# Routing before the values, four marks a step, eight early splits: one change to a fused attention and mixture kernel

## The chip, the cores and the metric

The kernel runs on one core of a Trainium2 chip. The metric is device time in microseconds (us). TensorE is called PE below, VectorE DVE, ScalarE ACT, GpSimd POOL, and SyncE SP.

## The reference, cut to what matters

```
scores = where(0 <= i - j < 64, q k^T / 8, -1e9);  x = softmax(scores) v           # B=4, H=8, S=576, D=64
x -> [2304, 512];  noisy = x @ w_gate + log1p(exp(x @ w_noise)) * noise             # 8 experts
top 2 of noisy per token, softmax of the two -> top2_w
y = sum over the two of top2_w * (relu(x @ w1[e]) @ w2[e])                           # w1 512x1024, w2 1024x512
h = y @ w_in;  g = h if h >= 1, 0 if h <= -1, else (h + 1)^2 / 4;  out = g @ w_out   # w_in 512x2048
```

## The kernel before, in words

There are 18 tiles of 128 tokens. A tile is cut into two units, so attention has 36 units and the loop at its heart calls `step(u)` for u = 0 to 36. One step writes down work of several units, and each engine executes its share in the order in which it is written (`manual_schedule`: nothing is reordered). In an even step PE gets the scores of the next tile (L282 mask, L291), the transposes of an older tile's output (`Ex`, L347), the transposes of the unit's probabilities (`C`, L313), the products (`place`, L557) and the 32 matmuls of probabilities and values (`Dm`, L327). In an odd step it gets `C`, `place` and the gate logits (`Gm`, L365). DVE has the row maxima (`top`, L298, two in an even step), the division of the values by their sums (in `Dm`, L332, L333 and L335, which makes the tile `x`), the routing, and the subtraction that splits a weight chunk into a high and a low part (`split_w`, L148; ACT makes the high part at L147).

Routing goes by groups of six tiles. `route(g)` is a generator: `advance` runs it up to a `yield` of 1 or 2, and then the rest waits for the next step. Its pieces are the noisy logits (L426 to L450), the largest eight and their indices (L454, L457), the one-hot choices (L460 to L478), the positions (PE, L482 to L486: how many tokens before this one chose the same expert), the slot numbers (L491 to L505) and then twelve pairs of marks a group: `ohr` (L510, DVE) and `ohe` (L517 on DVE for odd tiles, L520 on ACT for even ones). `MARKS` says how many pairs one call of `advance` takes. `place` in the next call multiplies each pair on PE (L557) and adds the product to one PSUM tile, the list of token numbers by expert.

After the 24 products of the first two groups, `early` reads that list (L385 to L401), and POOL gathers three blocks of 128 rows (`xg0a`, L650) with which expert 0 starts while the third group is still routed. The blocks are transposed (L672) and split (L675 ACT, L676 DVE `xlo0a`) behind steps 35 and 36. Then the experts run: `mm1` (L763), `act_relu` (L769 ACT, L770 DVE `hl`), `mm2` (L803), by weight chunks. `tail` routes the third group between the chunks of expert 0, two calls a chunk, then makes the rest of the list (`finish_ids`) and gathers the other two blocks of expert 0 (`xg0b`); the first block of expert 1 (`xge`) is gathered at the first chunk of the unit `0b`.

`EW` weight chunks are loaded and split during attention, half a chunk a step, one every `LS` steps; `SPLITS[0]` splits the next ones at chunks `F0` and on of expert 0. Three `raw` tiles take the loads.

```
n_early = 2 * gstart[EARLY]                              # 24 products
calm = 2 if g < EARLY - 1 else 0                         # in route: groups 1 and 2 go on at once
if state["first"] or nids[0] < n_early: return           # in early
for b in range((0, 1, NA)[max(u - NU + 2, 0)]):          # behind steps 35 and 36
    if ("0a", b) in gat: xpose("0a", b, NA, Sb[b])
```

Of the kernel before, what the change touches and what calls it, by code (L numbers as in the profile page):

```python
# [28 lines left out]
NT = N // P  # L29
# [6 lines left out]
GROUPS = [6, 6, 6]  # L36
EARLY = 2
NA = 3
MARKS, TAIL = (2, 6), 6
Y0, LOOK = 3, 1  # L40
PTB = 3
EW, L0, LS, F0 = 10, 1, 3, 4
G2 = [2, 4, 4, 4, 4]
NCE = E * NF
MID = N // 2
# [8 lines left out]
def fused_kernel(ctx, tc, qT, kT, v, wg, noise, wcat, out, wd=None):  # L54
# [17 lines left out]
    att, rte, ffn = ExitStack(), ExitStack(), ExitStack()  # L72
    wk = rte.enter_context(tc.tile_pool(name="wk", bufs=2, side="right"))
    gp = rte.enter_context(tc.tile_pool(name="gp", bufs=2, side="right"))
    oh = rte.enter_context(tc.tile_pool(name="oh", bufs=8, side="right"))
    ac = rte.enter_context(tc.tile_pool(name="ac", bufs=1, side="right"))
    qk = att.enter_context(tc.tile_pool(name="qk", bufs=2))
    vp = att.enter_context(tc.tile_pool(name="vp", bufs=4))
# [125 lines left out]
    for s in (0, 64):  # L204
        nc.gpsimd.affine_select(out=id64[s:s + 64, :], in_=id64[s:s + 64, :], compare_op=ALU.not_equal, fill=1.0,
                                base=0, pattern=[[-1, 64]], channel_multiplier=1)
        m = m0[s:s + 64]
# [94 lines left out]
    def soft(u):  # L302
        sb, nb = Sb[u % 3], mxs.pop(u)
        p = wk.tile([P, 4, P], F32, tag="p", name=f"p{u}", bufs=4)
        for g in range(4):
            nc.scalar.activation(p[:, g, :], sb[:, g * P:g * P + P], AF.Exp, bias=nb[:, g:g + 1], scale=0.125)
        pr[u] = p
# [106 lines left out]
    def route(g):  # L414
# [40 lines left out]
        yield calm  # L455
        for a in range(T):
            nc.vector.max_index(out=ix[:, a, :], in_max=mx8[:, t0 + a, :], in_values=ny[:, a, :])  # L457
        yield calm
        ixf = tl("ixf", [P, T, 2])
        nc.vector.tensor_copy(ixf, ix[:, :, 0:2])  # L460
        yield 0
# [130 lines left out]
    def logits(i, u):  # L592
        Gm(i, u)
        g, t = tile_group[i]
        if t == GROUPS[g] - 1:
            live.append(route(g))
            next(live[-1])

    def step(u):
        for c in range(EW):  # L600
            if u == L0 + LS * c:
                load_raw(c)
        if u + 2 < NU:
            if (u + 2) % 4 == 0 and (u + 2) // 4 + 1 < NT // 2:
                load_qk((u + 2) // 4 + 1)
                keys_before((u + 2) // 4 + 1)
            if (u + 1) % 2 == 0 and (u + 1) // 2 + 1 < NT:
                load_v((u + 1) // 2 + 1)


        m = u // 2
        if u % 2 == 0:
            if u + 2 < NU:
                A(m + 1)
            if 0 <= m - 2 < NT:
                Ex(m - 2, u)
        if u < NU:
            C(u)
        if u % 2 == 0 and u + 2 < NU:
            top(u + 2)  # L620
            top(u + 3)
        if u + 2 < NU:
            soft(u + 2)
        place()
        early()
        if 0 <= u - 1 < NU:
            Dm(u - 1)
        if u % 2 == 1 and 0 <= m - 2 < NT:
            logits(m - 2, u)
        advance(MARKS[u > NU - 10])  # L630

        for c in range(EW):
            for h in range(2):
                if u == L0 + LS * c + 3 + h:
                    split_w(c, h)
            if u == L0 + LS * c + 4 and c >= EW - 2:
                load_raw(c + 2)
# [57 lines left out]
    def tail():  # L695
        logits(NT - 2, NU + 1)
        Ex(NT - 1, NU + 1)
        advance(TAIL)
        yield
        logits(NT - 1, NU + 1)  # L700
        while live or oq or pq:
            place()
            advance(TAIL)
            yield
        finish_ids([(NA, NB), (0, NA), (NB, E * JB)])
        count()
        rte.close()
        pool["xp"] = ffn.enter_context(tc.tile_pool(name="xp", bufs=2, reuse_waits="tile", side="right"))
        for b in range(units[1]["nb"]):
            prep_gather(units[1], b)  # L710
            yield

    def count():
        cnt = bank[6][:, CNT:CNT + E]
# [248 lines left out]
    for s in range(len(seq)):  # L963
        ui, n = seq[s]
        un = units[ui]
        f = n - un["ch"][0]
        nxt = units[ui + 1] if ui + 1 < len(units) else None
        last = f == len(un["ch"]) - 1
        decode = 1 < ui < E and 1 <= f <= 6
        lag = (7 if ui == FIRST2 else 3) if un["e"] is None else 0  # L970
        if ui == 0:
            more()
        if s == NF:
            dyn["e"] = nc.values_load(cnt_i[0:1, 1:2], engines=[mybir.EngineType.SP], min_val=0,
                                      max_val=(E - 1) * NF)
            choice_weights()
        if ui == 1 and f == 2:
            overflow(nc.values_load(cnt_i[0:1, 0:1], min_val=0, max_val=N))
            pool["rd"] = dec.enter_context(tc.tile_pool(name="rd", bufs=2, reuse_waits="tile"))
        if ui == SPILL and f == 0:  # L980
            dec.close()
            pool["last"] = ffn.enter_context(tc.tile_pool(name="wlast", bufs=1, reuse_waits="tile"))
        if ui == U7A and f == 0:
            xT["7b"] = [t[:, :, G2[0] * P:] for t in xT["7a"]]

        if ui == SPILL - 1:
            ahead = [(units[SPILL], 0, 0)] + [(units[U7A], b, b + 1) for b in range(NB)]
        elif ui == U7B:
            ahead = [(nxt, b, Y0 + b) for b in range(nxt["nb"])]
        else:  # L990
            ahead = [(nxt, b, b + lag) for b in range(nxt["nb"])] if ui and ui not in (SPILL, U7A) and nxt else []
        for x, b, w in ahead:
            if f == w:
                prep_gather(x, b)

        def ahead_xpose():
            for x, b, w in ahead:
                if f == w + 2 + (un["e"] is None):
                    prep_xpose(x, b)
        if decode and ndec < min(ndl, n64):  # L1000
            dec_a(ndec)
        if un["e"] is None:
            ahead_xpose()
        for x, b, w in ahead:
            if f == w + 1:
                fill.append(lambda x=x, b=b: prep_mix(x, b))
        while fill and un["e"] is not None:
            fill.popleft()()

        while ndone < min(s + 2 + (ui >= FIRST2 and LOOK), len(seq)):  # L1010
            do_mm1(ndone)
            ndone += 1
        if ui == 0:
            more()
            if f == NF - 2:
                for _ in rest:
                    pass
                for b in range(nxt["nb"]):
                    prep_xpose(nxt, b, (TR, bank[6])[b])
        if un["e"] is not None:  # L1020
            ahead_xpose()
        while fill:
            fill.popleft()()
        do_mm2(s)
        for _ in range(SPLITS[ui][f] if ui in SPLITS else int(0 < ui < SPILL)):
            if nsplit < NCH:
                split_w(nsplit)
                nsplit += 1
            if nload < NCH:
                load_raw(nload)  # L1030
                nload += 1
        if decode:
            if ndec < min(ndl, n64):
                dec_b(ndec)
                ndec += 1
            if ndl < n64:
                dec_load(ndl)
                ndl += 1
# [34 lines left out]
```

## Time and profile before

| | |
|---|---|
| median of three runs | 1016.88 us (1015.85 to 1021.69) |
| profiled execution, its own time | 1017.2 us |
| its span (first to last instruction) | 1015.5 us |
| mean granted TensorE clock | 0.987 |
| PE busy | 987.3 us (97%) |
| DVE, ACT, POOL busy | 573.8 (57%), 417.7 (41%), 197.7 us (19%) |

The span is what lies between the first and the last instruction; 1.7 us of the execution's own time lie around it. Busy shares are means over attention, expert 0 and everything after, three stages with different limits, so the stages are read apart. PE's clock has two levels, 1.2 and 2.4 GHz; a granted clock of 0.50 in a stretch is the lower one throughout.

### The profile page before, as it was taken

Reading aid. Unit: us, or ns where it says so; the run is one execution under the profiler, and the core shown is the slowest. Engines: PE = TensorE matmul, PEld = TensorE weight load, DVE = VectorE, ACT = ScalarE, POOL = GpSimd, SP = SyncE. Lnnn points to the kernel's source line nnn. Section 1 sums busy time; section 2 is a strip of 40 time slices with the busy share of each in tenths; the row PEclk is TensorE's granted clock in tenths of the full one; section 3 lists DMA queues with packets and bytes.
Section 4 is the critical chain, followed back from the end, with each engine's and each line's share of the span. In section 5 each row is a group of like instructions: output and inputs, shape, how many; then the busy total and the mean of one; then the engine's idle time right before and its main releaser. Section 6 shows DMA issues by size and latency. Waiting matters only on the chain.

```text
span 1015.5 us, 16345 instructions
## 1 busy us (share of the span) xinstructions
PE 987.3 (97%) x6373; PEld 853.9 (84%) x6374; DVE 573.8 (57%) x1112; ACT 417.7 (41%) x811; POOL 197.7 (19%) x257
## 2 busy tenths in 40 slices
PE   8987899999999999999999999999999999999998
PEld 5876778999999999999987999888888888888886
DVE  4687465567675757665443656645445544545443
ACT  6886424444444544443334544424223322422221
POOL 3221103223324343432312111102001000200000
PEclk9998799999999999999999999999999999999999
DMA  8875305556666666677433643020020002001001
GB/s 253 283 238 188 105 21 183 180 178 192 211 210 199 205 203 202 189 219 258 139 102 121 219 148 92 21 83 22 0 104 21 1 1 105 21 1 41 1 1 42
DMA packets 50048, 127.01 MB, mean 125 GB/s; under 512 B 5296, under 2 KB 15792, under 8 KB 49968
## 3 DMA queue, kind: packets, MB, share of 16 engines
q1 hardware_dynamic: 39616, 93.94, 30.1%
q0 software_dynamic: 9056, 29.63, 7.8%
q10 hardware_dynamic: 1296, 2.36, 0.6%
q8 instruction: 51, 0.84, 0.3%
q14 instruction: 29, 0.24, 0.1%
HBM read 97.47 MB, written 28.44 MB: 124 GB/s over the span
## 4 chain that ended last, share of the span: by engine, by line
PE 86%; DVE 1%; DMA 0%; POOL 0%; ACT 0%; issue 0%; another core or an unknown queue 0%; POOLq 0%; ACTq 0%
PE bank L763 42%; PE bank L803 41%; PE bank L672 2%; PE bank L830 1%; DMA xge<-x_dram,src_i 0%; PE bank L841 0%; PE bank L365 0%; PE ob L327 0%; POOL y_dram L792 0%; POOL xg0a L650 0%; PE bank L347 0%; DVE hl0a L770 0%; PE bank L557 0%; PE bank L313 0%; ACT hh0a L769 0%
## 5 line engine op out<-in xcount | busy, mean ns | idle before, releaser
L803 PE MATMUL bank<-w,hhg 128*128 128x512 f32 x576 | 178.2, 390 | 0.0
L803 PE MATMUL bank<-w,hhe 128*128 128x512 f32 x480 | 151.0, 396 | 0.0
L763 PE MATMUL bank<-xhig,w 128*128 128x512 f32 (+1 forms) x640 | 149.2, 375 | 0.0
L763 PEld LDWEIGHTS bank<-xhig,w 128*128 128x128 f32 x640 | 112.4, 188 | 22.5
L148 DVE TENSOR_TENSOR w<-raw,w 128x1024 fp32r<-128x1024 f32 (+1 forms) x90 | 99.5, 1106 | 52.0 <-ACT w L147 49.0
L763 PE MATMUL bank<-xhie,w 128*128 128x320 f32 x768 | 128.5, 309 | 0.0
L803 PEld LDWEIGHTS bank<-w,hhg 128*128 128x128 f32 x576 | 107.2, 188 | 23.1
L763 PEld LDWEIGHTS bank<-xhie,w 128*128 128x128 f32 x768 | 118.7, 188 | 3.8
L803 PE MATMUL bank<-w,hlg 128*128 128x512 f32 x288 | 112.4, 390 | 0.0
L779 DVE TENSOR_SCALAR m<-r 128x512 f32<-128x512 f32 (+1 forms) x80 | 32.2, 402 | 130.1 <-ACT r L776 130.0
L782 ACT ACTIVATE hhg<-r 128x512 fp32r<-128x512 f32 (+1 forms) x80 | 47.2, 590 | 134.8 <-DVE r L781 130.5
L776 ACT ACTIVATE r<-bank 128x512 f32<-128x512 f32 (+1 forms) x80 | 44.5, 556 | 140.9 <-PE bank L763 140.8
L770 DVE SCALAR_TENSOR_TENSOR hle<-bank,hhe 128x320 fp32r<-128x320 f32 x96 | 47.0, 490 | 98.1 <-ACT hhe L769 95.6
L803 PEld LDWEIGHTS bank<-w,hhe 128*128 128x128 f32 x480 | 87.1, 188 | 15.6
L803 PE MATMUL bank<-w,hle 128*128 128x512 f32 x240 | 93.7, 391 | 0.0
L769 ACT ACTIVATE hhe<-bank 128x320 fp32r<-128x320 f32 x96 | 41.8, 436 | 125.1 <-PE bank L763 117.2
L147 ACT ACTIVATE w<-raw 128x1024 fp32r<-128x1024 f32 (+1 forms) x90 | 87.3, 971 | 13.2 <-PE bank L803 10.8
L783 DVE TENSOR_TENSOR hlg<-r,hhg 128x512 fp32r<-128x512 f32 (+1 forms) x80 | 56.1, 702 | 58.8 <-ACT hhg L782 58.8
L763 PE MATMUL bank<-xlog,w 128*128 128x512 f32 (+1 forms) x320 | 80.5, 373 | 0.0
L891 POOL TENSOR_TENSOR y<-y 128x512 f32<-128x512 f32 x16 | 25.7, 1605 | 247.0 <-ACT y L890 245.5
L763 PE MATMUL bank<-xloe,w 128*128 128x320 f32 x384 | 71.9, 309 | 0.0
L183 POOL TENSOR_TENSOR dt<-rawd 128x512 f32<-128x512 f32 x32 | 33.2, 1037 | 175.7 <-DVE rawd L181 159.7
(244 smaller groups left out, 1491.7 us busy)
## 6 DMA issues: line engine op xcount, KB each, us to landing
raw<-wcat SPq DMA_DIRECT2D x64, 512.0 KB, 4.2
rawd<-wd SPq DMA_DIRECT2D x32, 512.0 KB, 4.5
w2f<-dt POOLq DMA_DIRECT2D x32, 256.0 KB
raw<-w2f SPq DMA_DIRECT2D x16, 512.0 KB, 3.5
y<-y_dram SPq DMA_DIRECT2D x16, 512.0 KB, 4.7
vE<-v SPq DMA_DIRECT2D x18, 260.0 KB, 4.5
x_dram<-x SPq DMA_DIRECT2D x18, 256.0 KB, 2.4
k<-kT SPq DMA_DIRECT2D x8, 512.0 KB, 6.4
```

What stands on the lines that cost most here:

```text
L147: nc.scalar.activation(w[:, 0, c], t[:, c], AF.Copy)
L148: nc.vector.tensor_tensor(out=w[:, 1, c], in0=t[:, c], in1=w[:, 0, c].bitcast(F32), op=ALU.subtract)
L183: nc.gpsimd.tensor_tensor(out=t.bitcast(F32), in0=hf, in1=lf, op=ALU.add)
L763: nc.tensor.matmul(ps, lhsT=l[:, k * P:k * P + P], rhs=r[:, k, s:s + w], start=(c == 0), stop=(c == len(prods) - 1))
L769: nc.scalar.activation(hh, ps, AF.Relu)
L770: nc.vector.scalar_tensor_tensor(out=hl, in0=ps, scalar=0.0, in1=hh.bitcast(F32), op0=ALU.max, op1=ALU.subtract)
L776: nc.scalar.activation(r, ps, AF.Relu, bias=1.0)
L779: nc.vector.tensor_scalar(out=m, in0=r, scalar1=0.5, scalar2=1.0, op0=ALU.mult, op1=ALU.min)
L782: nc.scalar.activation(hh, r, AF.Copy)
L783: nc.vector.tensor_tensor(out=hl, in0=r, in1=hh.bitcast(F32), op=ALU.subtract)
L803: nc.tensor.matmul(M2[b], lhsT=l[:, sl], rhs=r[n], start=(first and a == 0), stop=(last and a == 2))
L891: nc.gpsimd.tensor_tensor(out=y2, in0=y2, in1=y1, op=ALU.add)
```

## The change

`MARKS` and `TAIL` fall: in the last ten steps and in `tail`, `advance` takes four pairs of marks a call instead of six. `EW` falls from 10 to 8 and `LS` rises from 3 to 4: eight chunks are split during attention, at other steps, and five instead of three at chunks 2 to 6 of expert 0. In `step`, the logits come before `place`, and `advance` comes before `Dm`. `route` gets a stop behind the indices for the groups 1 and 2. The pool of marks has ten buffers a kind instead of eight. The first block of expert 1 is gathered at the end of `tail`.

```diff
-MARKS, TAIL = (2, 6), 6
+MARKS, TAIL = (2, 4), 4
-EW, L0, LS, F0 = 10, 1, 3, 4
+EW, L0, LS, F0 = 8, 1, 4, 2
-    oh = rte.enter_context(tc.tile_pool(name="oh", bufs=8, side="right"))
+    oh = rte.enter_context(tc.tile_pool(name="oh", bufs=10, side="right"))
...
             nc.vector.max_index(out=ix[:, a, :], in_max=mx8[:, t0 + a, :], in_values=ny[:, a, :])
-        yield calm
+        yield 2
...
+        if u % 2 == 1 and 0 <= m - 2 < NT:
+            logits(m - 2, u)
         place()
         early()
+        advance(MARKS[u > NU - 10])
         if 0 <= u - 1 < NU:
             Dm(u - 1)
-        if u % 2 == 1 and 0 <= m - 2 < NT:
-            logits(m - 2, u)
-        advance(MARKS[u > NU - 10])
...
             prep_gather(units[1], b)
             yield
+        prep_gather(units[2], 0)
...
-            if f == w:
+            if f == w and (x["key"], b) not in gat:
                 prep_gather(x, b)
```

The first place is DVE in an even step of attention (step 24). The rows L332 to L335 divide the values, L510 and L517 make marks. Before:

```order
L298 TENSOR_REDUCE mx_1435<-bank_74 128x4
L298 TENSOR_REDUCE mx_1439<-bank_72 128x4
L332 TENSOR_SCALAR rl_1466<-ob 128x8
L333 RECIPROCAL rl_1466<-rl_1466 128x8
L335 TENSOR_TENSOR x_1469<-ob,rl_1466 128x512
L510 TENSOR_SCALAR ohr_3_0_1473<-io_178,rf_1275,tcode_183 128x128
L517 TENSOR_SCALAR ohe_3_0_1475<-io_178,rf_1275 128x145
L510 TENSOR_SCALAR ohr_3_1_1477<-io_178,rf_1275,tcode_183 128x128
L517 TENSOR_SCALAR ohe_3_1_1479<-io_178,rf_1275 128x145
```

And the same step now:

```order
L298 TENSOR_REDUCE mx_1421<-bank_74 128x4
L298 TENSOR_REDUCE mx_1425<-bank_72 128x4
L510 TENSOR_SCALAR ohr_3_0_1436<-io_178,rf_1266,tcode_183 128x128
L517 TENSOR_SCALAR ohe_3_0_1438<-io_178,rf_1266 128x145
L510 TENSOR_SCALAR ohr_3_1_1440<-io_178,rf_1266,tcode_183 128x128
L517 TENSOR_SCALAR ohe_3_1_1442<-io_178,rf_1266 128x145
L332 TENSOR_SCALAR rl_1460<-ob 128x8
L333 RECIPROCAL rl_1460<-rl_1460 128x8
L335 TENSOR_TENSOR x_1463<-ob,rl_1460 128x512
```

The marks, which need nothing of this step's values, have moved ahead of the three operations that wait for PE.

The second place is POOL from the end of attention to the start of expert 1: `vE` is the copy of values that the next tile's `Dm` needs, `xg0a` the early gathers, `y_dram` the scatters of expert 0's first three blocks. Before:

```order
L299 TENSOR_SCALAR nb_1954<-mx_1953 128x4
L650 DMA xg0a_1974<-x_dram,src_i 128x512
L650 DMA xg0a_1976<-x_dram,src_i 128x512
L650 DMA xg0a_1978<-x_dram,src_i 128x512
L340 COPY vE_1598<-vE_1710 64x520
L340 COPY vE_1710<-vE_1866 64x520
L745 DMA xg0b_2437<-x_dram,src_i 128x512
L745 DMA xg0b_2455<-x_dram,src_i 128x512
L792 DMA y_dram<-y0a_2564,dst_i 23040x512
L792 DMA y_dram<-y0a_2571,dst_i 23040x512
L792 DMA y_dram<-y0a_2578,dst_i 23040x512
L745 DMA xge_0_2598<-x_dram,src_i 128x512
```

And now:

```order
L299 TENSOR_SCALAR nb_1899<-mx_1898 128x4
L340 COPY vE_1584<-vE_1696 64x520
L651 DMA xg0a_2015<-x_dram,src_i 128x512
L651 DMA xg0a_2017<-x_dram,src_i 128x512
L651 DMA xg0a_2019<-x_dram,src_i 128x512
L340 COPY vE_1696<-vE_1810 64x520
L747 DMA xg0b_2463<-x_dram,src_i 128x512
L747 DMA xg0b_2481<-x_dram,src_i 128x512
L747 DMA xge_0_2497<-x_dram,src_i 128x512
L794 DMA y_dram<-y0a_2562,dst_i 23040x512
L794 DMA y_dram<-y0a_2569,dst_i 23040x512
L794 DMA y_dram<-y0a_2576,dst_i 23040x512
```

The early gathers stand one copy, which is two steps, later (in step 34 instead of step 32), and the first gather of expert 1 has moved ahead of the three scatters.

## Rows read from the trace of the kernel before

**Rows 1.** Windows by stage: stretch, length, busy of PE, PEld, DVE, ACT, POOL, clock, DMA.
```profile
60.00:85.00 25.00, 20.13 (x293) 17.29 (x291) 17.68 (x57) 18.31 (x53) 4.85 (x14) 0.86 0.66 213
85.00:123.00 38.00, 29.74 (x391) 25.54 (x391) 24.37 (x101) 19.85 (x53) 6.87 (x13) 0.78 0.35 117
123.00:165.00 42.00, 40.12 (x229) 35.46 (x230) 25.27 (x106) 11.78 (x24) 2.07 (x3) 1.00 0.21 63
...
175.00:1015.50 840.50, 833.91 (x4464) 723.11 (x4462) 465.50 (x739) 317.51 (x543) 158.50 (x152) 1.00 0.35 114
```
**Rows 2.** Waits of PE, first 180 us: total, times, longest.
```profile
PE bank L557 <- DVE ohe L517: 3.9, 7, 1.1
...
PE bank L672 <- DMA xge<-x_dram,src_i: 1.4, 1, 1.4
PE bank L482 <- DVE ohs L467: 1.3, 2, 1.1
```
**Rows 3.** Timeline of PE, steps 23 to 36: start, length, operation, idle before it.
```profile
69.56 0.22 PE L557 MATMUL bank<-ohe,ohr 128*128 128x145 f16 x1 [1.07 <-DVE ohe L517]
...
71.19 1.04 PE L291 MATMUL bank<-k,qbuf 64*64 64x128 f32 x32
...
78.07 1.92 PE L291 MATMUL bank<-k,qbuf 64*64 64x128 f32 x32
...
85.63 0.41 PE L282 MATMUL bank<-mask,id 64*64 64x512 bf16 x4
...
90.34 0.41 PE L282 MATMUL bank<-mask,id 64*64 64x512 bf16 x4
...
99.64 1.58 PE L557 MATMUL bank<-ohe,ohr 128*128 128x145 f16 x6 [4.08 <-DVE ohr L510]
...
110.30 0.63 PE L347 MATMUL bank<-idn,x 128*128 128x128 f32 x4
...
113.75 1.15 PE L327 MATMUL ob<-vE,pt 128*64 128x65 f32 x32 [2.20 <-POOL vE L340]
...
120.77 1.17 PE L672 MATMUL bank<-idr,xg0a 128*128 128x128 f32 x8
123.03 1.62 PE L763 MATMUL bank<-xhi0a,w 128*128 128x384 f32 x8 [1.08 <-DVE xlo0a L676]
```
**Rows 4.** Timeline of DVE: a mark of step 22, maxima of step 32, the early list.
```profile
68.42 0.69 DVE L335 TENSOR_TENSOR x<-ob,rl 128x512 f32<-128x512 f32 x1
69.03 0.31 DVE L510 TENSOR_SCALAR ohr<-io,rf,tcode 128x128 f16<-128x128 f16 x1
...
105.57 1.29 DVE L298 TENSOR_REDUCE mx<-bank 128x4 f32<-128x512 f32 x2
107.78 0.46 DVE L385 COPY first<-bank 128x290 f32<-128x290 f32 x1 [0.92 <-PE bank L557]
```
**Rows 5.** Window of a long stretch of low clock, columns as in rows 1.
```profile
114.00:121.00 7.00, 7.00 (x86) 6.48 (x81) 2.01 (x6) 1.79 (x3) 0.61 (x1) 0.56 0.32 119
```
**Rows 6.** Window of DVE alone, from step 28's maxima to the last early mark.
```profile
87.05:104.97 17.92, 14.56 (x70) 0.80 0.31 107
```
**Rows 7.** Timeline of POOL: gathers.
```profile
109.34 1.21 POOL L650 DMA_INDIRECT xg0a<-x_dram,src_i  x1 [2.10 <-DVE rl L332]
...
112.12 0.94 POOL L650 DMA_INDIRECT xg0a<-x_dram,src_i  x1 [0.30 <-issue]
...
149.47 0.99 POOL L745 DMA_INDIRECT xg0b<-x_dram,src_i  x1 [0.30 <-issue]
...
168.77 1.55 POOL L745 DMA_INDIRECT xge<-x_dram,src_i  x1 [0.30 <-issue]
```
**Rows 8.** Chain of waits: the first gather of expert 1, issue to landing.
```profile
168.77 4.96 DMA xge<-x_dram,src_i
```
**Rows 9.** Timeline of PE and DVE, end of expert 0's first unit and a split.
```profile
158.92 0.80 PE L672 MATMUL bank<-idr,xg0b 128*128 128x128 f32 x8
...
168.23 1.23 DVE L148 TENSOR_TENSOR w<-raw,w 128x1024 fp32r<-128x1024 f32 x1 [0.52 <-issue]
```

## The prediction, made before the changed kernel was run

> **What bounds the kernel now.** I read the windows by stage first [rows 1]. From 175 us to the end PE is busy for 833.91 of 840.50 us at full clock: nothing in the change touches that stage but the split chunks it starts with, so I carry it over unchanged. What can move is the first 175 us. From 60 to 85 us PE is busy for 20.13 of 25 us with a mean clock of 0.86, and from 85 to 123 us for 29.74 of 38 us at 0.78: there PE waits, and runs slowly between the waits. In expert 0 (123 to 165 us) it misses 1.88 us.
>
> The table of PE's waits and its timeline say for what [rows 2, 3]. In step 23 PE stands 1.07 us before a product, until DVE has made the mark `ohe`, and the same happens in steps 25 and 27; with the second product of each pair (0.17 us) that is 1.23 us three times. Before the products of step 31 it stands 4.08 us. Before the values of step 34 it stands 2.20 us, for a copy that POOL makes behind the three early gathers. Expert 0 starts at 123.03 us.
>
> The reason for the three equal waits is on DVE [rows 4]: the mark at 69.03 us is made behind `x` (68.42 us), and `x` waits for PE's values of the same step, while PE's next products wait for the mark. It is a ring from PE through DVE to PE, once in two steps.
>
> The clock has two levels here [rows 3, 5]. The 32 score matmuls take 1.04 us at 71.19 us and 1.92 us at 78.07 us, on the lower level. The granted clock is 0.56 from 114 to 121 us, behind the wait of 2.20 us.
>
> **The change part by part.**
>
> *Routing ahead of the values (steps up to 27).* The marks of an even step now stand behind the maxima, so they are done while PE is still at the transposes and values; the logits ahead of `place` give another microsecond. No new wait: behind the marks `x` comes about 1.3 us later on DVE, but its next reader, the transposes two steps later, has over 4 us. I take away 3 x 1.23 = 3.7 us. The low clock around 78.07 us should go with the wait at its start; it lasts some 3.4 us there, and what takes 1.92 us takes 1.04 at full clock, so 1.6 us. Bounds for the clock: 0 to 1.6; I take 1.6, since no wait of PE is left in front of it. Term 1: -5.3.
>
> *Four pairs a step and the stop behind the indices (steps 28 to 34).* Two limits. PE: a pair of steps without marks and waits takes 4.71 us (85.63 to 90.34 us [rows 3]); three of these, twelve products at 0.15 (six took 1.58 at 99.64 us, on the lower clock), the positions at some 0.3 and two groups of transposes ahead of the last products (0.63 each, as at 110.30) end at 85.63 + 14.1 + 1.8 + 0.3 + 1.25 = 103.1 us in the old time. DVE: from 87.05 to 104.97 us it does 14.56 us of work [rows 6]; up to the last early mark there now come two more maxima (1.29 [rows 4]), one more `x` (0.69, some 1.05 with its sums) and half a split (0.6, half of 1.23 [rows 9]), with the gaps between 70 instructions some 18.1 us, so it ends at 105.2 us if it never rests. Here DVE is the longer one, and PE will wait for marks again, a microsecond or so in steps 32 to 34, instead of 4.08 at once. The list was complete at 107.78 us [rows 4]; I take 105.5, a gain of 2.2. Bounds: 4.6 (PE's limit), and a loss of 3.8, if the steps keep the old pace (step 34 began at 110.30 us [rows 3], and its two transposes take 1.25). Term 2: -2.2.
>
> *The early gathers two steps later.* In step 32 they had four more steps to hide behind; now they have two. From the complete list (107.78) to the start of expert 0 (123.03) it took 15.3 us. Now: 1.6 us to the first gather (107.78 to 109.34 [rows 4, 7]); the third is issued 2.8 us after the first (112.12); it lands 4.96 us after its issue, if it takes what the gather of expert 1 took [rows 8]; and from the last transposes to expert 0 it is 2.3 us (120.77 to 123.03 [rows 3]). Together 11.6 us, a gain of 3.7: of the work PE had in between, two steps are now done before. The wait of 2.20 us for the copy of `vE` goes, because one copy stands ahead of the gathers now and the other has until step 36; in its place PE waits some 2 to 3 us for the first block to land, and I leave the low clock that followed the old wait in, since the new wait is as long. Bounds: PE's own work on this stretch is about 7.2 us, a gain of 8.1; a landing 2 us later leaves 1.7. Term 3: -3.7.
>
> The Trainium skill ("DMA: Bandwidth & Descriptors", Anatomy of one DMA) puts a POOL-issued transfer at 2.0 us plus its bytes over 436 GB/s, an estimated 2.6 us for a block of 256 KB. By that, term 3 would be 2.4 us larger; the row says 4.96, under other loads, and I go by the row.
>
> *The third group in `tail`.* PE's wait for the positions (most of the 1.3 us for `ohs` [rows 2]) goes, since a call of `mm1` now lies between them; with the waits for six marks at once, 1.88 us were missing in rows 1. But the routing takes one chunk (two calls, some 4 us) longer, so the list's second reading and the gathers `xg0b` come that much later, and two more splits (1.23 us each [rows 9]) stand in DVE's queue ahead of the routing. I expect one wait of 0.8 us for the first four marks behind a split and one of about 0.5 us before the transposes of `xg0b`. Cover of these now: the second gather is issued at 149.47 us [rows 7] and used at 158.92 [rows 9]; with 4.96 us to land, 4.5 us are spare, and the later start takes nearly all of that. Term 4: -0.5, between -1.9 and +3.
>
> A gather that ran beside a split took longer: 1.55 us at 168.77 us, beside the split that began at 168.23, against 0.94 to 0.99 for others [rows 7, 9]. The Trainium skill says why ("SBUF — State Buffer", SBUF: two separate sides): DVE with two SBUF inputs and POOL lock each other out of a shared port. It speaks against more splits in the stage that gathers, and would make term 4 up to 1.2 us worse; but in the order the splits stand behind `hl`, and the two gathers run beside the list's operations, as before, when they took 0.99. So I add nothing.
>
> *Eight early splits.* Four half splits fewer in attention: none of PE's waits up to step 27 is for a split [rows 2], so I give them nothing there, and in steps 28 to 34 they are in term 2. The two that move to expert 0 are hidden by PE's work, some 5 us a chunk (40.12 us for eight [rows 1]). Ten buffers cost nothing.
>
> *First gather of expert 1.* It was issued at 168.77 us behind three scatters, and PE stood 1.4 us for it [rows 2, 8]. Issued before them it has landed some 8 us earlier. Late next is nothing that the trace shows: the following gathers move up by one place. Term 5: -1.4, bounds 0 and -1.4.
>
> Sum: -5.3 - 2.2 - 3.7 - 0.5 - 1.4 = -13.1 us. The profiled execution took 1017.2 us, so 1004.1; it stands 0.3 above the median of the runs, and I say 1004.0.
>
> **The rivals.**
>
> *DVE is the bound.* The marks' ring goes, but DVE has 17.92 us with 14.56 us of work in it, and the waits of steps 28 to 34 come back one by one, each with low clock. Then term 1 is 3.7, term 2 nothing, term 3 is 2, the tail nothing: -7.1, 1010. For it speaks rows 6; against it, that the waits now fall behind four marks and not six.
>
> *PE never rests.* The gathers land quickly, the clock stays high, and the limits of PE decide: terms of 5.3, 4.6, 6, 1.9 and 1.4 make -19, 998. Against it: rows 8.
>
> *Slower: the early gathers on the path.* Place: the transposes behind step 35. In step 32 the chain from list to landing (9.3 us) lay beside four steps of PE's work; two steps are about 5.5 us, so from now on each microsecond by which the list is late makes the kernel a microsecond longer. With the old pace the list is complete at 111.6 us and expert 0 starts at 123.2, as before; 5 us slower in all needs a list at about 118 us, even if half of the other terms hold. Such would be DVE's 18 us becoming 31, for instance by marks on ACT held behind the exponentials. Price: 6 us, 1023. Rows 6 speak against it.
>
> *It does not do what it says.* The products might wait for ACT's marks rather than DVE's, or the waits move to the tail whole: 1015, no change. The row names `ohe` on DVE (L517), which is what moves, so this is unlikely.
>
> **How the numbers follow.** Forecast 0.57 (its own range 1000 to 1008), DVE the bound 0.17, PE never rests 0.14, no change 0.08, slower 0.04. The measurement can tell about 0.5% from no change, 5.1 us, so faster is below 1011.8: all of the forecast and of the third, and most of the second (0.13): 0.84. Same takes the rest of the second and the no change: 0.12. Slower 0.04. For 8 times in 10 the range must go to 998 on one side and take in the second case with its spread on the other: 998 to 1012.
>
> **What would show it.** Right: no wait of a microsecond before products in steps 23, 25 and 27; no 4.08; a wait of 2 to 3 us before the first transposes of `xg0a`, and none for `vE`; expert 0 starting at 111 to 113 us; no wait for `xge`; the stage from expert 1 on as long as before. Wrong: if expert 0 starts after 118 us, or if the transposes of `xg0b` wait for more than 2 us, my terms 2 to 4 are mistaken; if the clock falls in steps 26 to 33 without a wait before it, term 1's reading of the clock is.

## The result, and the profile after

The changed kernel takes 1003.52 us (median of 4 runs, 1001.91 to 1005.7), against 1019.29 us for the kernel before in the same comparison (4 runs, 1015.85 to 1021.95): a ratio of 0.9859, 95% interval 0.9825 to 0.9893. Its profiled execution took 1002.0 us with a span of 1000.3 us (before: 1017.2 and 1015.5). The forecast was 1004.0 us.

Where the 15.2 us of span came from I read by cutting both traces at the same places in the program, beginning with the step 22 (its mask products, L282), the step 28, the moment at which DVE copies the complete list (`first`, L385), expert 0's first product, the end of the transposes of `xg0b`, and the first product behind the transposes of `xge`:

| stretch, us | before | after | gained | predicted |
|---|---|---|---|---|
| up to step 22 | 62.83 | 62.47 | 0.36 | 0 |
| steps 22 to 27 | 22.80 | 16.75 | 6.05 | 5.3 (term 1) |
| step 28 to the list | 22.15 | 21.36 | 0.79 | 2.2 (term 2) |
| list to expert 0 | 15.25 | 10.89 | 4.36 | 3.7 (term 3) |
| expert 0 to the end of `xg0b`'s transposes | 36.69 | 34.51 | 2.18 | 0.5 (term 4) |
| from there past `xge` | 16.28 | 14.68 | 1.60 | 1.4 (term 5) |
| the rest | 839.50 | 839.64 | -0.14 | 0 |

The median lies 0.5 us from the forecast, and every sign is right, but that closeness is partly luck. Between the profiled executions, from which the sum was built, the gain is 15.2 us and not 13.1, and the two terms that were mis-sized most, 2 and 4, were missed in opposite directions (1.4 us too much, 1.7 us too little). First the windows of the changed kernel, cut by stage (columns as in [rows 1]), to lay beside [rows 1]:

```profile
60.00:85.00 25.00, 23.57 (x438) 20.61 (x433) 21.82 (x70) 21.96 (x67) 5.82 (x16) 1.00 0.70 225
85.00:111.00 26.00, 22.45 (x268) 19.15 (x260) 20.09 (x84) 14.87 (x40) 5.92 (x10) 0.74 0.46 153
111.00:146.00 35.00, 34.32 (x200) 30.75 (x201) 23.18 (x103) 11.22 (x23) 2.90 (x3) 1.00 0.29 90
160.66:1000.30 839.64, 833.03 (x4459) 722.46 (x4457) 465.35 (x739) 318.12 (x543) 157.92 (x152) 1.00 0.36 114
```

In the first stage PE is now busy for 23.57 of 25 us at full clock. In the second it still loses 3.5 us and has a mean clock of 0.74, so the low clock did not leave the kernel; it moved. In expert 0 PE misses 0.7 us.

What PE waits for in the first 180 us of the changed kernel (us in total, times, longest), to lay beside [rows 2]:

```profile
...
PE bank L482 <- ACT pt L315: 1.6, 2, 1.3
...
PE bank L535 <- DVE first L385: 1.1, 1, 1.1
PE bank L557 <- DVE ohe L517: 1.1, 3, 0.5
...
```

The marks' 3.9 us in seven waits are 1.1 us in three, and the wait for `xge` is not there. New are 1.3 us for `pt` in step 31 and 1.1 us at the count (L535, in step 34). PE's timeline shows where they lie, and what the clock did (to lay beside [rows 3]):

```profile
68.59 0.22 PE L557 MATMUL bank<-ohe,ohr 128*128 128x145 f16 x1 [0.53 <-DVE ohe L517]
...
79.07 0.22 PE L557 MATMUL bank<-ohe,ohr 128*128 128x145 f16 x1 [0.38 <-DVE ohe L517]
79.22 0.41 PE L282 MATMUL bank<-mask,id 64*64 64x512 bf16 x4
...
90.41 0.20 PE L482 MATMUL bank<-ohs,tri 128*128 128x48 bf16 x1 [1.33 <-ACT pt L315]
...
91.13 1.92 PE L291 MATMUL bank<-k,qbuf 64*64 64x128 f32 x32
...
101.08 0.16 PE L535 MATMUL bank<-Cn,ones 128*128 128x1 bf16 x1 [1.10 <-DVE first L385]
...
105.66 0.75 PE L673 MATMUL bank<-idr,xg0a 128*128 128x128 f32 x4
...
111.47 1.66 PE L765 MATMUL bank<-xhi0a,w 128*128 128x384 f32 x8 [0.69 <-ACT xhi0a L676]
...
131.72 0.22 PE L557 MATMUL bank<-ohe,ohr 128*128 128x145 f16 x1 [0.17 <-DVE ohe L517]
...
145.18 0.80 PE L673 MATMUL bank<-idr,xg0b 128*128 128x128 f32 x8
...
158.90 0.46 PE L673 MATMUL bank<-idr,xge 128*128 128x128 f32 x4
```

The reader is to see three things. Of the three waits of a microsecond in steps 23, 25 and 27, two are left, of 0.53 and 0.38 us, and no score products at 1.92 us follow them. Expert 0 starts at 111.47 us, inside the 111 to 113 that was named. And the first transposes of `xg0a` (105.66) have no wait in front of them, where 2 to 3 us were predicted: the experiments below take that up.

### The profile page after: what moved, and what is told of

It reads as the page before. It is cut to its first block, busy times and chain, and to the rows that moved or that the text cites. A ratio compares the mean times of both kernels' runs of the same rounds, so it can differ in the third digit from the quotient of the medians.

```text
span 1000.3 us, 16346 instructions
## 1 busy us (share of the span) xinstructions
PE 983.0 (98%) x6373; PEld 851.1 (85%) x6374; DVE 575.1 (57%) x1110; ACT 417.7 (42%) x809; POOL 198.2 (20%) x257
## 4 chain that ended last, share of the span: by engine, by line
PE 84%; ACT 0%; issue 0%
PE bank L765 41%; PE bank L805 40%; PE bank L673 2%; PE bank L832 1%; PE bank L843 0%; ACT hh L835 0%; ACT yg L810 0%; PE bank L823 0%
```

## The experiments

The traces of 13 kernels, the changed one twice, are cut at the same places. "The rest" takes 835.4 us in one group of runs and 838.8 to 840.3 us in another, whatever the kernel (more on that at the end), so the kernels are compared by these stretches, and by ratios to the kernel before on the same chip:

| kernel | 22 to 27 | 28 to list | list to e0 | 28 to e0 | e0 to `xg0b` | past `xge` |
|---|---|---|---|---|---|---|
| before | 22.80 | 22.15 | 15.25 | 37.40 | 36.69 | 16.28 |
| changed | 16.75 | 21.36 | 10.89 | 32.25 | 34.51 | 14.68 |
| order alone | 16.88 | 19.53 | 15.74 | 35.27 | 36.69 | 16.30 |
| all but the order | 21.18 | 22.82 | 12.03 | 34.85 | 34.45 | 14.64 |
| ten splits | 17.31 | 21.69 | 10.95 | 32.64 | 33.90 | 14.63 |
| six marks a step | 16.74 | 20.51 | 12.28 | 32.79 | 34.44 | 14.58 |
| count later | 16.75 | 21.36 | 11.19 | 32.55 | 34.50 | 14.64 |
| positions elsewhere | 16.55 | 21.77 | 10.66 | 32.43 | 34.48 | 14.63 |
| both of these | 16.56 | 22.22 | 11.28 | 33.50 | 36.29 | 14.63 |
| changed, again | 16.76 | 21.37 | 10.73 | 32.10 | 34.48 | 14.64 |
| splits sooner | 17.32 | 18.96 | 11.05 | 30.01 | 34.49 | 14.66 |
| tail back | 16.75 | 21.36 | 10.96 | 32.32 | 38.02 | 14.60 |
| gather alone | 22.79 | 22.13 | 15.02 | 37.15 | 36.66 | 14.63 |
| no stop | 16.74 | 21.32 | 11.02 | 32.34 | 34.50 | 14.59 |

"28 to list" does not always end in the same step: the list is read in step 32 in the kernel before, with the gather alone and with the order alone, in step 33 with six marks and without the stop, and in step 34 in the others. Across these groups "28 to e0" is the column to compare.

### The order alone, and everything but the order

The first kernel is the one before with the five calls of a step in the new order and nothing else; the second is the changed kernel with the old order.

```
 first:   logits(m - 2, u); place(); early(); advance(MARKS[u > NU - 10]); Dm(u - 1)
 second:  place(); early(); Dm(u - 1); logits(m - 2, u); advance(MARKS[u > NU - 10])
```

Expected of the first:

> The kernel before with one edit: in a step the logits come first, then the products, the early part and the routing, and the values last. Theory A (the ring of PE's values, DVE's division and DVE's marks is what cost the 6.0 us of steps 22 to 28): the waits of 1.06 us before the products of steps 23, 25 and 27 go, steps 22 to 28 (score masks of step 22 to those of step 28) take about 17 us instead of 22.8, and the kernel is 6 to 9 us faster. Rival B (what went is work: fewer half splits and marks a step): the three waits stay near 1 us and the kernel is within 2 us of before.

Expected of the second:

> The changed kernel with the order inside a step put back (products, early part, values, logits, routing); four marks, the stop, eight splits and the early gather stay. Theory A: the waits of about 1.06 us are back, steps 22 to 28 take about 22 us, and of the 15.2 us some 9 remain (about 1008 us). Rival B: steps 22 to 28 stay near 17 us, and nearly all of the gain remains (about 1004).

Measured: 1005.89 us for the order alone (ratio 0.993, 0.9914 to 0.9946), 1007.02 us for all but the order (0.9947, 0.9931 to 0.9962). The order alone shortens steps 22 to 27 to 16.88 us, and leaves expert 0's stage and `xge` as they were (36.69, 16.30). The total for all but the order falls short of its expectation: some 6 us of gain remain there (1013.23 us for the kernel before), where some 9 were expected. Without the order the three waits are back in PE's timeline of the second kernel:

```profile
71.22 0.22 PE L557 MATMUL bank<-ohe,ohr 128*128 128x145 f16 x1 [1.97 <-DVE ohe L517]
...
77.78 0.22 PE L557 MATMUL bank<-ohe,ohr 128*128 128x145 f16 x1 [1.06 <-DVE ohe L517]
...
84.33 0.22 PE L557 MATMUL bank<-ohe,ohr 128*128 128x145 f16 x1 [1.07 <-DVE ohe L517]
...
115.14 0.75 PE L673 MATMUL bank<-idr,xg0a 128*128 128x128 f32 x4 [4.35 <-DMA xg0a<-x_dram,src_i]
```

So the ring from PE through DVE and back is shown, by taking the order away and by making it alone. The order alone also keeps the wait for POOL's copy (2.0 us at L327) and the list's old place, and its stretch from list to expert 0 is the old one, 15.74 us: the gain there needs the other edits, with which the gathers come two steps later; no run moved the gathers alone.

### Ten early splits, and six marks a step

```
 ten splits:  EW, L0, LS, F0 = 10, 1, 3, 4     # changed: 8, 1, 4, 2
 six marks:   MARKS, TAIL = (2, 6), 4          # changed: (2, 4), 4
```

> The changed kernel with the ten early splits put back (EW, L0, LS, F0 = 10, 1, 3, 4). Theory A: steps 22 to 28 stay within 1 us of 16.75; four more half splits lengthen DVE's full stretch before the list, so the list is complete 0.5 to 2 us later and the kernel loses 0 to 2 us. Rival B: 4 us or more are lost, in steps 22 to 28.

> The changed kernel with six pairs of marks a step in attention again (the tail keeps four). If DVE's work is what bounds steps 28 to 34 (theory C), the same marks are made in two steps instead of three and the list is read two steps earlier, in step 34 still or in step 33: the products wait for marks again, 1 to 3 us at once, but expert 0 starts within 1.5 us of 111.5. If spreading the marks is what counts (rival D), a wait of 3 us or more with low clock behind it returns and expert 0 starts 3 us later or more.

Measured: 1001.43 us (ratio 0.9903, 0.9871 to 0.9935) and 997.46 us (0.9858, 0.9826 to 0.989). Neither differs from the changed kernel (0.9859) by more than the intervals allow. The two splits that the change moves into expert 0 cost 0.6 us there (34.51 against 33.90). Six marks a step bring the list 0.85 us sooner and expert 0 not at all (32.79 against 32.25 us from step 28). The list is read a step earlier there, so PE has more work left behind it; PE stands 1.86 us at the count, works at a granted clock of 0.59 from the list to expert 0, and waits for no block. In this kernel PE's own slow work, and not a landing, sets expert 0's start.

### The count behind its copy, and the wait in step 31

Two waits in the changed kernel had not been foreseen, 1.10 us at the count and 1.33 us in step 31. The next kernels move them: the count's product behind the values of the same step, and the positions' sums into a buffer that does not wait for `pt`.

```
 count later:           state["bump"] = True, and behind Dm(u - 1):
                        if state.pop("bump", False): live.append(bump()); next(live[-1])
 positions elsewhere:   pos = (OB[:, 0, :] if g < EARLY else bank[0])[:, POS:POS + T * E]
```

> The changed kernel, with the one matmul that counts expert 0's tokens (L535) written behind the values of step 34 instead of ahead of them. In the changed kernel PE stood 1.10 us at it, the clock was low from 100 to 111 us, and the gathers were never waited for. Theory E (that wait brings the low clock, and the slow work is what covers the gathers): the wait goes, PE reaches the first transposes at full clock some 3 us earlier and now waits 1 to 3 us for the first block; the stretch from step 28 to expert 0 gets 0 to 2 us shorter than 32.25. Rival F (the gathers are not near the path): no wait for the block, and the stretch is 4 us shorter or more.

> The changed kernel with the positions written to free columns of the values' PSUM tile instead of the bank whose transposes ACT has still to copy out. Theory: the wait of 1.33 us in step 31 goes, and with it the low clock of step 32. If PE's path sets the list (theory G), the stretch from step 28 to expert 0 is 2 to 3 us shorter than 32.25. If DVE, busy without a pause from 80 to 100 us, sets it (theory C), it is less than 1 us shorter.

> The changed kernel with both of these edits: the count behind the values, the positions in the values' PSUM tile. If theories C and E hold, expert 0 starts 0 to 2 us earlier after step 28 than in the changed kernel and the kernel is within 0.3% of it; if F and G hold, 5 us earlier and 0.5% faster.

Measured, one run each: 1002.93 us and 1001.63 us; both edits together 1005.34 us (4 runs; 0.9884, 0.984 to 0.9929). PE's timeline with the count later:

```profile
102.93 0.19 PE L535 MATMUL bank<-Cn,ones 128*128 128x1 bf16 x1
...
107.26 0.75 PE L676 MATMUL bank<-idr,xg0a 128*128 128x128 f32 x4 [2.52 <-DMA xg0a<-x_dram,src_i]
...
112.69 1.66 PE L768 MATMUL bank<-xhi0a,w 128*128 128x384 f32 x8 [1.16 <-DVE xlo0a L680]
```

The wait at the count is gone, and a wait of 2.52 us for the first gathered block stands in its place; from list to expert 0 it takes 11.19 us, no less than 10.89 (0 to 2 us less were expected). So the count's wait cost nothing: PE would have stood for the block. The theory that the chain from list to landing bounds this stretch (E in the expectations) holds for this kernel, its rival (F) falls.

With the positions elsewhere:

```profile
90.43 0.18 PE L482 MATMUL ob<-ohs,tri 128*128 128x48 bf16 x1 [2.48 <-DVE x L335]
...
105.27 0.54 PE L673 MATMUL bank<-idr,xg0a 128*128 128x128 f32 x4 [2.27 <-DMA xg0a<-x_dram,src_i]
```

The wait did not go, though that was expected: the 1.33 us for ACT became 2.48 us for DVE's `x`. But the low clock behind it went. The clock stayed at 1.00 from 84 to 104 us in this kernel (0.83 in the changed one), and yet the list came no sooner (21.77 us from step 28, against 21.36): the low clock does not decide when the list is ready. That speaks for DVE (theory C) and against PE's own pace (G), though the longer wait may hide a part. Both edits together are worse in the trace, and outside what either pair of theories expected (0 to 2 us or 5 us earlier; it is 1.25 us later): the wait for the block grows to 3.57 us, 33.50 us pass from step 28 to expert 0, and the clock is low in expert 0's first products, so that its stage takes 36.29 us (a granted clock of 0.81 from 113.90 to 120.00 us).

With the two smaller waits gone, PE only comes sooner to the block that it must wait for.

### The changed kernel again

> The changed kernel itself, on the same chip as the others: the same 1.4% below before within 0.3%, and from step 28 to expert 0 32 to 33 us.

Run beside the last three, with no edit: 1002.29 us against 1016.97 us for the kernel before (0.9867, 0.9818 to 0.9915). Its stretches repeat those of the first profile within 0.2 us, which is the measure for the table above.

### Splits sooner, and no stop behind the indices

If DVE sets the list, then taking splits out of the steps before it must bring it sooner. The first kernel spaces the eight splits by three steps rather than four, so that the four half splits of steps 28, 29, 32 and 33 move ahead of step 27; the second leaves out the stop behind the indices for the second group, so that its positions come a step sooner.

```
 splits sooner:  EW, L0, LS, F0 = 8, 1, 3, 2
 no stop:        yield 2 if g != EARLY - 1 else 0
```

> The changed kernel with the eight early splits three steps apart instead of four (LS = 3): the last half split is in step 26 and none in steps 28 to 33, where DVE never rests. Theory C+E (DVE up to the list, then the gathers, set the start of expert 0): up to the list DVE has four half splits of 0.6 us less to do, the list is complete about 19 to 19.5 us after the start of step 28 instead of 21.4, and the stretch from step 28 to expert 0 is 1.5 to 2.5 us shorter than 32.2; steps 22 to 28 get up to 1 us longer. Rival G (PE's path sets it): the stretch stays within 0.5 us of 32.2.

> The changed kernel without the stop behind the indices for the second group (the third keeps it), so its positions come a step sooner. If DVE sets the list, the list is complete within 1 us of 21.4 us after step 28 although it is read a step sooner; PE waits 2 us or more for the marks of steps 31 to 33, and the stretch from step 28 to expert 0 is 0 to 3 us longer than 32.2, since less of PE's work is done before the list.

Measured: 997.08 us (5 runs; before there 1012.59; ratio 0.9848, 0.9828 to 0.9869), and one run of 998.79 us. With the splits sooner the list stands 2.4 us earlier from step 28 (18.96), and expert 0 2.2 us. DVE's row of the list's copy, PE's of the block, and the window from step 28 to the list:

```profile
100.95 0.46 DVE L385 COPY first<-bank 128x290 f32<-128x290 f32 x1 [0.32 <-PE bank L557]
...
106.49 0.75 PE L673 MATMUL bank<-idr,xg0a 128*128 128x128 f32 x4 [2.39 <-DMA xg0a<-x_dram,src_i]
```

```profile
81.99:100.95 18.96, 17.22 (x292) 14.69 (x292) 17.92 (x81) 15.46 (x49) 3.05 (x9) 1.00 0.49 158
```

The stretch and DVE's busy time in it (20.33 us of 21.36 in the changed kernel, see term 2 below) fall by 2.4 us both, and DVE's idle time stays at 1.0 us. Three half splits fewer fall into the window, some 1.8 us; most of the rest is L443 and L467, which take 0.63 us less (see the end). So DVE's queue decides the list, and the list decides expert 0, where PE does not have more to do behind it, as with six marks. One thing the edit does not part: it moves ACT's halves of these splits too (ACT is busy for 15.46 us instead of 17.44); that DVE and not ACT is the limit rests on DVE's idle time. In the whole time little of it is seen. Steps 22 to 27 take 0.57 us more, and step 22 begins at 64.67 us, where two other kernels on that chip with the new order and four steps between splits began at 63.48 and 63.76; that start moves by 0.9 us between the two profiles of the changed kernel (62.47 and 63.34), so it is not shown that the splits make it later. The ratio cannot be told from the changed kernel's.

Without the stop the list is where it was (21.32 us), and PE's waits only change their names; those for marks are 1.4 us in all, where 2 us or more were expected:

```profile
PE bank L673 <- DMA xg0a<-x_dram,src_i: 1.5, 1, 1.5
PE bank L557 <- DVE ohe L517: 1.4, 5, 0.5
PE bank L482 <- DVE ohs L467: 1.3, 1, 1.3
```

### The tail's third group, and the gather alone

The first kernel is the changed one with the tail's old rules; the second is the kernel before with the first gather of expert 1 ahead of the scatters.

```
 tail back:      MARKS, TAIL = (2, 4), 6   and   yield 2 if g < EARLY else 0
 gather alone:   the kernel before, with prep_gather(units[2], 0) at the end of tail
```

> The changed kernel with the tail put back: six pairs a call there and no stop behind the indices for the third group. If these two make the gain of 2.2 us in expert 0's first unit, its length (start of expert 0 to the end of the transposes of xg0b) goes from 34.5 back to 36.5 us or more; if the splits at other chunks make it, it stays near 34.5.

> The kernel before with the first gather of expert 1 moved to the end of the tail, and nothing else. PE's wait of 1.4 us for it goes, the stretch from the transposes of xg0b to the next chunk's products goes from 16.3 to 14.7 us, and nothing else moves. If the wait was the branch behind the overflow test and not the gather, the stretch stays above 16.

Measured, one run each: 1002.57 us and 1011.42 us (before there 1012.59). With the tail's old rules expert 0's stretch is 38.02 us and not 34.5. Windows of that stretch, first of the kernel with the old tail, then of the changed one:

```profile
112.83:150.85 38.02, 35.69 (x200) 31.18 (x201) 23.81 (x103) 10.87 (x22) 2.90 (x3) 1.00 0.30 85
```

```profile
111.47:145.98 34.51, 34.30 (x200) 30.73 (x201) 22.89 (x102) 10.78 (x22) 2.90 (x3) 1.00 0.29 89
```

PE does the same 200 matmuls. It idles 2.33 us instead of 0.21, and it is "busy" 1.39 us longer. Most of that can be placed: the twelve products of the marks (L557) cover 2.72 us in the timeline instead of 1.70, since with the old rules several start one by one, each behind its mark, and no longer overlap. The waits of this stretch with the old tail:

```profile
PE bank L482 <- DVE ohs L467: 1.1, 1, 1.1
PE bank L557 <- DVE ohe L517: 0.6, 4, 0.2
PE bank L557 <- DVE ohr L510: 0.5, 1, 0.5
```

So the new rules of the tail are worth 3.5 us. The two more splits in that stage cost 0.6 us by the kernel with ten splits, or 1.3 us if the old tail is compared with the kernel before (38.02 against 36.69); no run says which.

The gather alone takes the last stretch from 16.28 to 14.63 us and moves none of the others in the table by more than 0.3 us. The rival that its wait was the branch behind the overflow test falls with that. That edit is worth 1.65 us by itself.

## Why the prediction was right, step by step

**What bounds the kernel.** Right. PE bounds it, and what could move lay in the first 175 us: the rest took 839.64 us against 839.50.

**Term 1, the order (-5.3 predicted, -6.05 measured).** Right in its mechanism: two experiments show the ring. The sum was made of other parts than I gave. The windows of this stretch, of the kernel before and of the changed one:

```profile
62.83:85.63 22.80, 19.09 (x280) 16.25 (x276) 15.23 (x49) 16.00 (x46) 3.51 (x10) 0.85 0.69 218
```

```profile
62.47:79.22 16.75, 15.62 (x280) 13.45 (x277) 14.13 (x46) 14.03 (x42) 3.70 (x10) 1.00 0.77 246
```

PE's idle time fell from 3.71 to 1.13 us, by 2.6 and not by 3.7, mostly because 0.53 and 0.38 us of waits stay. Its busy time for the same 280 matmuls fell by 3.47 us, as the clock rose from 0.85 to 1.00; I had taken only the 1.6 us that I saw behind one of the waits. The other half of the low clock stood in step 22 and was not the ring's: PE waited 1.16 us for `pt` in step 21, and the clock behind it was 0.60.

```profile
62.83:67.00 4.17, 4.17 (x58) 3.48 (x56) 3.48 (x14) 2.62 (x8) 0.44 (x2) 0.60 0.88 259
```

How much of the 6.05 us is the order's is therefore not one number. With the order alone, the same wait for `pt` (1.15 us) stands before step 22 and the clock stays at 1.00; that kernel gains 5.92 us. In the kernel with all but the order the three waits are back, the first of them longer, and yet the clock of this stretch stays at 1.00; taking the order away cost 4.43 us there:

```profile
64.54:85.72 21.18, 16.30 (x280) 13.78 (x276) 14.78 (x48) 15.07 (x45) 3.44 (x10) 1.00 0.73 235
```

So the ring's idle time goes and comes with the order in each of these runs, and the low clock in some of them only. I had bounded this term at 5.3 us, and 6.05 lies beyond.

**Term 2, steps 28 to the list (-2.2 predicted, -0.79 measured).** The choice of DVE as the longer side was right, the size was not. The windows from step 28 to the list's copy, of the kernel before and of the changed one:

```profile
85.63:107.78 22.15, 17.15 (x242) 14.14 (x243) 17.03 (x76) 12.80 (x36) 2.50 (x8) 0.77 0.32 107
```

```profile
79.22:100.58 21.36, 18.66 (x292) 15.81 (x292) 20.33 (x84) 17.44 (x52) 3.23 (x9) 0.92 0.55 182
```

DVE is busy for 20.33 of 21.36 us: it has nothing more to give. My 18.1 us ran from step 28's maxima to the last early mark, and I added 0.3 us to the list. Measured, they are 19.07 (80.63 to 99.70 us) and 0.88. Two things were left out. One is the half split that stands directly in front of the list's copy, with a wait for ACT ahead of it:

```profile
99.97 0.69 DVE L148 TENSOR_TENSOR w<-raw,w 128x512 fp32r<-128x512 f32 x1 [0.27 <-ACT w L147]
100.58 0.45 DVE L385 COPY first<-bank 128x290 f32<-128x290 f32 x1
```

My sum holds one half split more than before, and the trace has that one ahead of the last mark (three against two); this fourth one I did not count, as I had not asked where in the queue the splits stand. The kernel with the splits sooner moved all four and took 2.4 us off this stretch. The other is that some of DVE's instructions ahead of the last mark became longer, by 1.2 us together (see the end). And PE did not wait for marks in steps 32 to 34, as I had said, but 1.33 us for `pt` in step 31, 0.53 us for `x` in step 34 and 1.10 us at the count.

**Term 3, list to expert 0 (-3.7 predicted, -4.36 measured).** The chain was right: list, indices, POOL, landing of the third block, transposes. The step on how it would look failed. I foresaw 2 to 3 us of waiting for the first block; the changed kernel shows 1.10 us at the count, unforeseen, and then PE at a clock of 0.53, which fills the time until the blocks have landed:

```profile
100.58:111.47 10.89, 9.57 (x93) 8.50 (x92) 5.43 (x20) 3.32 (x6) 3.75 (x4) 0.53 0.39 129
```

At its end PE's weight load stands for the third block:

```profile
110.03 0.44 PEld L673 LDWEIGHTS bank<-idr,xg0a 128*128 128x128 f32 x3 [0.32 <-DMA xg0a<-x_dram,src_i]
```

Seven of the variants show the predicted wait for the first block. In five of them (2.52, 2.27, 2.39, 2.38 and 1.54 us) the stretch is as long as in the changed kernel (10.66 to 11.19 us). One of the five is the kernel with the old tail, which is the changed kernel up to expert 0: whether PE stands or works slowly here differs from run to run, and the two cost about the same. In four of the five the third block had landed before PE came to it (without the stop it landed as PE came); there the first block's landing and PE's work behind it set expert 0's start, so the equal length is not the same chain each time. The wait for POOL's copy of `vE` is gone, as said. POOL's timeline shows the first and the third early gather, and those of the tail (to lay beside [rows 7]):

```profile
102.12 1.21 POOL L651 DMA_INDIRECT xg0a<-x_dram,src_i  x1 [5.60 <-DVE src_i L401]
...
104.91 0.95 POOL L651 DMA_INDIRECT xg0a<-x_dram,src_i  x1 [0.30 <-issue]
...
141.72 0.99 POOL L747 DMA_INDIRECT xg0b<-x_dram,src_i  x1 [0.30 <-issue]
143.11 0.94 POOL L747 DMA_INDIRECT xge<-x_dram,src_i  x1 [0.40 <-issue]
```

From the list's copy to the first gather it is 1.54 us (1.6 assumed), and from the first issue to the third 2.79 (2.8). The third block is used 5.12 us after its issue, as it lands (4.96 assumed), and expert 0 starts 1.44 us later (2.3 assumed): the term came out larger by this last link. Landings vary. The first block had landed 3.54 us after its issue, or sooner; in the variants where PE stood for it, it was used 3.86 to 4.21 us after issue, and 5.06 us with all but the order.

**Term 4, the tail (-0.5 predicted, -2.18 measured).** This is the term that was mis-sized most, and it lies beyond its bound of 1.9. The waits of 0.8 and 0.5 us that I set against the gain did not come: PE's only wait in that stage's routing is 0.17 us at 131.72. The second gather of `xg0b` is issued at 141.72 us and used at 145.18 without a wait, so it landed within 3.46 us and not 4.96. The gather beside a split, 1.55 us against "0.94 to 0.99 for others", was also read too narrowly: [rows 7] itself has a first gather of 1.21 us. The gain of the new rules, 3.5 us by the tail put back, was also larger than the 1.88 us that I could see as missing time, since part of it was counted as busy. The two more splits take back 0.6 to 1.3 us of it.

**Term 5, `xge` (-1.4 predicted, -1.60 measured).** Right, a little beyond my bound of 1.4, and the gather alone gives the same.

**The rivals.** "DVE is the bound" was half true: in steps 28 to 34 it is, and term 2 came to nearly nothing, but its waits did not come back in steps 22 to 27 nor in the tail. "PE never rests" fails on the 0.74 of clock in the second stage. "Slower" needed a list at 118 us; it came at 100.58.

## What to carry to other kernels

Where two engines hand work to each other in a ring, put the instruction that the other engine waits for ahead of the one that waits for the other engine; count what this saves from the window's idle time and from its granted clock apart: the clock was the larger half between these two kernels, and nothing in the kernel that only lacks the order. Where a chain through a DMA sets the end, a wait of the fast engine inside its shadow costs nothing, and the gain lies in the engine that makes the chain's first link: look at what stands in front of that link in its queue. A wait that the table of waits does not show may still sit inside busy time, so compare the busy time of the same instructions in two kernels.

## What the runs showed of the hardware

**A copy on POOL lengthens DVE's instructions beside it.** With the new order the routing stands where instructions on PE's results stood, and part of it starts together with POOL's copy of `vE`. DVE's rows in the changed kernel, then POOL's, then DVE's row of the kernel without the stop:

```profile
82.78 0.67 DVE L443 TENSOR_TENSOR w<-w,uu 128x48 f32<-128x48 f32 x1
...
89.32 0.67 DVE L467 TENSOR_TENSOR ohs<-o 128x48 bf16<-128x48 f32 x1
```

```profile
82.77 0.61 POOL L340 COPY vE<-vE 64x520 f32<-64x520 f32 x1 [0.55 <-POOL nb L299]
...
89.32 0.61 POOL L340 COPY vE<-vE 64x520 f32<-64x520 f32 x1
```

```profile
88.67 0.21 DVE L467 TENSOR_TENSOR ohs<-o 128x48 bf16<-128x48 f32 x1
```

In the kernel before both take 0.21 us. The mark `ohe` is 0.62 us instead of 0.26 at 67.92 and 78.40, beside copies at 67.81 and 78.28. That is some 0.3 to 0.46 us beside five of the six copies from 67.81 to 95.88 us, on the engine that sets the list. No run was made to take the copy away, but in two runs it fell elsewhere, and the lengthening went with it. Without the stop, L467 runs at 88.67 us, its copy comes at 91.47, and it takes 0.21 us again, while L443, at 83.79 us beside a copy of 83.78, still takes 0.67. With the splits sooner, L443 starts at 86.14 us as a copy begun at 85.54 ends, and takes 0.20. So the copy beside it makes the difference in these runs; by what means is argued and not shown. The Trainium skill ("SBUF — State Buffer", SBUF: two separate sides) describes an exclusive lock between POOL's instructions and those of DVE that run in a two-port mode or, against an instruction of POOL that reads SBUF, have two SBUF inputs, and says that the one that comes second blocks whole. The two rows, which have two inputs beside a copy that reads SBUF, agree with it: they end 0.06 to 0.07 us behind the copy. I had weighed the lock for the gathers alone, and not for DVE's own time.

**The low clock does not always follow the same wait.** Behind 1.33 us of waiting in step 31 the 32 score products took 1.92 us in the changed kernel, at a granted clock of 0.57 (90 to 94 us). In its second run, behind 1.32 us at the same place, they took 1.04 us. The kernel with all but the order says the same of the ring's waits (term 1). A forecast of the clock behind one wait is a chance, not a number.

**One wait, far behind the change, parts the runs into two groups.** The rest of the program, from expert 1 on, takes 835.45 us in the kernel without the stop:

```profile
161.65:997.10 835.45, 830.80 (x4459) 721.10 (x4457) 464.71 (x739) 315.66 (x542) 157.38 (x152) 1.00 0.36 114
```

The same 4459 matmuls take 839.64 us in the changed kernel's first profile. The clock is given as 1.00 for both, but a mean over 840 us hides a short fall. The traces part at one place, in the middle of the rest; PE's row there in the changed kernel:

```profile
526.28 0.65 PE L843 MATMUL bank<-w,hh 128*64 128x256 f32 x4 [1.82 <-ACT hh L835]
```

From 520 to 532 us the clock is 0.86 there. The kernel without the stop has no such wait, and a clock of 1.00 in that window. PE idles 1.96 us longer in the changed kernel's rest, which is this wait but for a little, and is busy 2.23 us longer, of which the low clock explains some 1.7 (an estimate: 0.14 of 12 us). The kernel before has the same wait, and so have the four profiles of the comparison with 1016.97 us (1.82 to 1.88 us; 838.8 to 840.3 us for the rest); the eight profiles on two other chips, at 835.4 us, do not. Why ACT is late there no run shows, and chip and time of the runs changed together. The difference is larger than what most edits above are worth, which is why they are read by stretches.
